# Weight conversion and attention in the first token group of a three-stage kernel: a piece converted within one pair of blocks

## The chip, the cores and the metric

The kernel runs on one core of one Trainium2 chip. The metric is the device time of one execution in microseconds (us), as the median over several runs.

## What is computed

Three stages follow one another; the input is attention's q, k, v (4 batches, 8 heads, 576 rows, head size 64), so 2304 tokens of 512 numbers.

```python
kv = np.einsum('bhsd,bhse->bhde', k, v)
out = np.einsum('bhsd,bhde->bhse', q, kv)
rms = np.sqrt(np.mean(out * out, axis=-1, keepdims=True) + 1e-06)
x = out / rms * g_norm                     # then reshaped to (2304, 512)

h = x @ w_in                               # 512 x 2048
g = h * np.clip(h + 3.0, 0.0, 6.0) / 6.0
x = g @ w_out                              # 2048 x 512

logits = x @ w_gate                        # 8 experts, the largest wins
h = np.maximum(np.einsum('ecd,edf->ecf', disp, w1), 0.0)
y = np.einsum('ecf,efd->ecd', h, w2)       # then weighted by the gate
```

`disp` holds the tokens sorted by expert, 576 places for each. `w_in` and `w_out` come as 64-bit floats, the rest as 32-bit ones.

## The kernel before, in words

**Number format.** A matrix value is split into two 16-bit halves (hi and lo), and a product is three TensorE products (hi·hi, hi·lo, lo·hi). So every weight must first be converted. `w_in` is converted in eight pieces of 256 columns, here called p0 to p7, `w_out` in eight pieces of 256 rows, p8 to p15 (`conv[0]` to `conv[15]` in the code). `f64_piece` (L217) converts one piece in six steps, each a step of a generator: three integer operations on VectorE (DVE; L228, L231, L234) that make a 32-bit float `f` out of the two words of the 64-bit one, then two on ScalarE (ACT; L239 writes the hi half, L241 scales `f` in place), and one on GpSimd (POOL; L243 writes the lo half). After the third step `feed()` issues the next load of a piece on SP's queue (L98). `convert(i, n)` (L621) issues the next n steps of piece i.

**Token groups.** The 2304 tokens go in five groups of 512 (the last has 256). For a group, `mm1` makes 16 blocks h of 128 columns (24 TensorE products of 512 columns for a pair of blocks, L572); `gated` (L575) turns each block into g on three engines: ACT reads the block from PSUM into t (L580), DVE multiplies (L582, g6), ACT writes g's hi half (L584), and POOL its lo half (L585; DVE does it in the later groups). `mm2` (L592) then multiplies g by w_out, 12 products a block and 512 tokens (L600). A pair of blocks f = 2k, 2k+1 of `mm1` needs p(k), one of `mm2` needs p(8+k).

**The first group.** Its code (up to `early.close()`, L698) stands under a manual schedule: each engine executes its instructions in the order in which the code was written. After that only SP's order is manual. In the first group all sixteen pieces are converted, at each even f half of two pieces: DVE's three steps of one piece (`convert(kf + 2, 3)`), and ACT's and POOL's three of the piece whose DVE steps ran a pair earlier (`convert(kf + 1, 3)`), L664 and L665 in the first loop and L685 and L686 in the second. After the first group come the other four groups, which convert nothing of these two matrices, and the experts.

**Attention.** The first 512 rows of batch 0 are done by `first_group` (L322 to L415): TensorE products `o`, ACT's squares, TensorE sums (`ss`), a chain of small DVE operations (L371 to L376), the products `r`, which spread the norms to all rows (L386), and then ACT's `x0T` (L395). `warm` issues products of zeros (L644) for TensorE's clock. All other rows are done by `att_o` (L419) in parts: products `o` (L436), ACT's square (L439), DVE's reduction (L440), DVE's `ms` (L445), ACT's square root (L450), four small DVE operations, DVE's `xs` (L468), ACT's and POOL's `row` (L480, L482), and a transposing DMA on SP (L483). `att_kv` makes the products k·v of a batch in PSUM, `keep_kv` (L306) copies them into the tile `kvbd` on DVE and ACT, `load_kv` and `load_q` issue a batch's loads on SP (L77 to L89).

Of the kernel before, what the change touches and what calls it, by code (L numbers as in the profile page):

```python
# [9 lines left out]
F32 = mybir.dt.float32  # L10
# [6 lines left out]
P = 128  # L17
# [13 lines left out]
def moe_chain(ctx: ExitStack, tc: tile.TileContext, qT, k, v, g_norm, w_in, w_out,  # L31
# [111 lines left out]
    for i in range(P // D):  # L143
        nc.sync.dma_start(gn[i * D : (i + 1) * D, :], g_norm.rearrange("(d o) -> d o", o=1))
    feed(3)
    load_kv(1)


    wg_raw = const.tile([P, NP, E], F32, name="wg_raw")
    nc.sync.dma_start(wg_raw, w_gate.rearrange("(c p) e -> p c e", p=P))  # L150
    bd = const.tile([P, NP, P], F32, name="kvbd")
    nc.gpsimd.memset(bd, 0.0)
    iota = const.tile([P, P], F32, name="iota")
# [12 lines left out]
    for i in range(2):  # L166
# [10 lines left out]
    wg = const.tile([P, NP, 2 * E], F16, name="wg")  # L177
    nc.scalar.activation(wg[:, :, :E], wg_raw, AF.Copy, scale=S_GATE)
    nc.vector.scalar_tensor_tensor(out=wg[:, :, E:], in0=wg_raw, scalar=S_GATE, in1=wg[:, :, :E],
                                   op0=ALU.mult, op1=ALU.subtract)  # L180
    xd = dram.tile([E * CAPP, ROW], F16, name="xd")
# [89 lines left out]
    with ExitStack() as p1:  # L271
# [33 lines left out]

        def keep_kv(ps):  # L306
            nc.vector.tensor_copy(bd[:D, :, :D], ps[:D, :, :D])
            nc.scalar.activation(bd[D:, :, D:], ps[D:, :, D:], AF.Copy)
# [13 lines left out]
        def first_group(w_a, w_b):  # L322
# [23 lines left out]
            for p in range(NP):  # L346
                ps = bank("o")
                nc.tensor.matmul(ps, bd[:, p, :], raws["q", 0, p // 2][:, p % 2, :T], start=True, stop=True)
                sq = sg.tile([P, T], F32, tag="g", name="sq0")
                nc.scalar.activation(sq, ps, AF.Square)  # L350
                banks.append(ps)
                sqs.append(sq)
            for _ in range(3):
                next(w_a)
            ss = bank("ss")
# [7 lines left out]
            nc.scalar.activation(u, ms, AF.Sqrt, bias=eps, scale=1.0 / D)  # L363
            next(w_a)
            next(w_a)
            for p in range(NP):
                oc = sg.tile([P, T], F32, tag="g", name="oc")
                nc.scalar.activation(oc, banks[p], AF.Copy)
                banks[p] = oc
            next(w_a)  # L370
            nc.vector.tensor_scalar(out=ms, in0=ms, scalar1=1.0 / D, scalar2=1.0e-6, op0=ALU.mult, op1=ALU.add)  # L371
# [4 lines left out]
            nc.vector.scalar_tensor_tensor(out=r, in0=q, scalar=-3.0, in1=r, op0=ALU.add, op1=ALU.mult)  # L376
            warm(14)
            warm(16)

# [27 lines left out]
            low(0, x0, nc.vector)  # L407
            low(1, x1, nc.gpsimd)
            x2 = norm(2)
            x3 = norm(3)  # L410
            low(2, x2, nc.vector)
            low(3, x3, nc.gpsimd)
            for _ in range(3):
                next(w_b)
# [4 lines left out]
        def att_o(b, parts, start=0):  # L419

            chunks, s0 = [], start
            while s0 < S:
# [151 lines left out]

        def gated(g, f, ps, eng):  # L575
            n_t = sizes[g]
            sc = S_G / (S_X0 * S_WIN)

            t = sb.tile([P, T], F32, tag="t", name="t")[:, :n_t]
            nc.scalar.activation(t, ps, AF.Relu, bias=b3, scale=sc / (S_X0 * S_WIN))  # L580
            g6 = sb.tile([P, T], F32, tag="g6", name="g6")[:, :n_t]
            nc.vector.scalar_tensor_tensor(out=g6, in0=t, scalar=6.0 * sc, in1=ps, op0=ALU.min, op1=ALU.mult)  # L582
            gt = sg.tile([P, 2, T], F16, tag="g", name="g")
            nc.scalar.activation(gt[:, 0, :n_t], g6, AF.Copy)  # L584
            eng.tensor_tensor(out=gt[:, 1, :n_t], in0=g6, in1=gt[:, 0, :n_t], op=ALU.subtract)  # L585
            gts[g].append(gt)
# [62 lines left out]
        warm(11, wb)  # L649
        keep_kv(att_kv(0, lambda: warm(8, wb)))  # L650
        nc.vector.tensor_scalar(out=gn, in0=gn, scalar1=S_WIN, scalar2=None, op0=ALU.mult)
# [10 lines left out]
        for f in range(NF):  # L662
            kf = f // 2
            if f % 2 == 0:  # L664
                convert(kf + 2, 3)  # L665
                convert(kf + 1, 3)
            if f > 1:
                ps = bank("h")
                mm1_mm(ps, 0, f, range(NP), PAIRS, True, True)
                hs.append(ps)  # L670
            gated(0, f, hs[f], nc.gpsimd)
            if f == 11:
                kv1 = att_kv(1)
            if f > 5 and f % 2 == 1:
                nc.sync.dma_start(*fills.pop(0))
        list(att_o(0, (1,), T))
        load_q(1)
        keep_kv(kv1)
        load_kv(2)
        acc = [bank("x") for _ in range(sizes[0] // P)]  # L680
        att1 = att_o(1, (2, 1, 1, 1))
        for f in range(NF):
            kf = NF // 2 + f // 2
            if f % 2 == 0:
                convert(kf + 2, 3)  # L685
                convert(kf + 1, 3)  # L686
            for j, ps in enumerate(acc):
                mm2(ps, 0, j, range(f, f + 1))
                if f == NF - 1:
                    finish_block(ps, 0, j)  # L690
            if 4 <= f <= 11:
                next(att1)
# [8 lines left out]
        for g in range(1, NG):  # L701
            for f in mm1(g):
# [6 lines left out]
                if f == 10 and g + 1 < B:  # L709
                    keep_kv(att_kv(g + 1))  # L710
                    if g + 2 < B:
# [253 lines left out]
```

## Time and profile before

| what | value |
|---|---|
| median of three runs | 702.54 us (702.40 to 704.43) |
| the profiled execution | 701.1 us |
| its span, first to last instruction | 699.3 us, mean granted TensorE clock 0.987 of full speed |
| TensorE (PE) busy in the span | 656.1 us (94%) |
| DVE, ACT, POOL busy | 340.3, 278.4, 107.3 us |

The first group takes four stretches of the span:

| stretch, us | what runs | PE busy | DVE busy | ACT busy |
|---|---|---|---|---|
| 0 to 31.19 | attention of the first 512 rows | 23.48 | 10.12 | 9.72 |
| 31.19 to 86.39 | `mm1`, with p2 to p9 converted on DVE | 48.72 | 44.54 | 36.92 |
| 86.39 to 146.45 | `mm2`, with p10 to p15 and batch 1's attention | 51.34 | 38.68 | 26.17 |
| 146.45 to 699.30 | groups 1 to 4, experts | 532.55 | 246.97 | 205.59 |

How the rows further down are read. A row of the timeline is: start in us, duration in us, engine, line and operation, tile out<-in with its shape, how many instructions of the kind ran in a row (x), and in brackets how long the engine had been idle and what ended that. PE is TensorE's products, PEld its weight loads, SPq the DMA queue of SP. A row of windows is: start:end, length, then busy us (and instructions) of PE, PEld, DVE, ACT and POOL, the granted clock of TensorE as a share of full speed, DMA's share, GB/s. A row of waits is: who waited, for whom, us in total, how often, the longest.

### The profile page before, as it was taken

What the parts mean: (1) busy time and instruction counts of PE and PEld (TensorE: products, weight loads), DVE (VectorE), ACT (ScalarE), POOL (GpSimd) and SP (SyncE); (2) the same over time, 40 slices, a digit from 0 to 9 for tenths busy, and PEclk for the clock granted to TensorE, in tenths of its full rate; (3) what the DMA queues carried; (4) which work ended last, traced back from release to release, by engine and by line L of the source; (5) the groups of instructions that cost most, each with busy time, mean ns of one, the idle gap of its engine ahead of it and who ended that gap; (6) DMA issues with size and microseconds to landing.
All of it is one profiled execution on the core that took longest, in us unless ns stands there. A gap on an engine that the chain in (4) does not pass through costs nothing. (4 is left out here: it accounts for less than half of the span.)

```text
span 699.3 us, 12621 instructions
## 1 busy us (share of the span) xinstructions
PE 656.1 (94%) x5071; PEld 374.9 (54%) x5071; DVE 340.3 (49%) x786; ACT 278.4 (40%) x433; POOL 107.3 (15%) x112
## 2 busy tenths in 40 slices
PE   7788969899899999999999999988998999999986
PEld 3333525444454445544444448556775766776754
DVE  1687785736582164732553029552134661166262
ACT  2457753535441154410443018431144561166171
POOL 1256652400010110001100011010011010110101
PEclk9989989999999999999999999999999999999998
DMA  9997879470628543362100115509839997089750
GB/s 308 355 265 214 252 247 317 124 202 15 181 62 194 173 131 130 113 143 46 47 16 1 31 45 162 150 24 147 214 71 287 296 211 194 32 196 255 241 109 23
DMA packets 125221, 108.78 MB, mean 156 GB/s; under 512 B 83943, under 2 KB 88551, under 8 KB 125152
## 3 DMA queue, kind: packets, MB, share of 16 engines
q1 hardware_dynamic: 122096, 98.42, 53.5%
q0 software_dynamic: 3056, 9.41, 3.7%
q8 instruction: 47, 0.77, 0.5%
q14 instruction: 22, 0.18, 0.1%
HBM read 64.55 MB, written 25.23 MB: 128 GB/s over the span
## 5 line engine op out<-in xcount | busy, mean ns | idle before, releaser
L572 PE MATMUL h<-x0T,w 128*128 128x512 f16 (+1 forms) x960 | 195.7, 362 | 9.8 <-POOL w L243 5.8
L600 PE MATMUL x<-w,g 128*128 128x512 f16 x864 | 194.1, 383 | 8.7 <-POOL w L243 6.4
L572 PEld LDWEIGHTS <-w 128*128 128x128 f16 x960 | 92.3, 98 | 102.9 <-issue 9.0
L600 PEld LDWEIGHTS <-g 128*128 128x128 f16 x864 | 83.9, 99 | 109.2 <-issue 15.0
L861 PE MATMUL h<-xe,w 128*128 128x128 f16 (+1 forms) x1920 | 107.2, 218 | 8.6 <-PEq L899 3.1
L876 PE MATMUL y<-w,ht 128*128 128x512 f16 (+1 forms) x504 | 112.3, 379 | 1.6 <-DVE ht L785 1.6
L861 PEld LDWEIGHTS <-w 128*128 128x128 f16 x1920 | 104.9, 99 | 15.2 <-issue 9.8
L876 PEld LDWEIGHTS <-ht 128*128 128x128 f16 (+1 forms) x504 | 48.9, 99 | 55.7 <-issue 1.7
L582 DVE SCALAR_TENSOR_TENSOR g<-t,h 128x512 f32<-128x512 f32 (+1 forms) x80 | 50.2, 632 | 40.4 <-ACT t L580 40.4
L866 DVE SCALAR_TENSOR_TENSOR ht<-h,ht 128x512 f16<-128x512 f32 (+1 forms) x40 | 26.5, 663 | 86.7 <-ACT ht L865 86.7
L580 ACT ACTIVATE t<-h,b 128x512 f32<-128x512 f32 (+1 forms) x80 | 51.2, 640 | 36.7 <-PE h L572 36.5
L584 ACT ACTIVATE g<-g 128x512 f16<-128x512 f32 (+1 forms) x80 | 46.2, 585 | 45.7 <-DVE g L582 45.4
L553 POOL DMA_INDIRECT xd<-row,sl x18 | 19.4, 1076 | 280.8 <-DVE sl L551 163.5
L259 DVE SCALAR_TENSOR_TENSOR w<-raw_kv,w 128x1024 f16<-128x1024 f32 x33 | 40.2, 1223 | 32.1 <-ACT w L256 31.5
L585 DVE TENSOR_TENSOR g<-g,g 128x512 f16<-128x512 f32 (+1 forms) x64 | 39.4, 623 | 27.0 <-ACT g L584 26.9
L887 POOL DMA_INDIRECT out<-ysb,ti x21 | 21.2, 1008 | 202.6 <-ACT ysb L886 85.8
L607 DVE SCALAR_TENSOR_TENSOR row<-x,row 128x512 f16<-128x512 f32 x18 | 12.3, 690 | 74.2 <-ACT row L606 74.2
L865 ACT ACTIVATE ht<-h 128x512 f16<-128x512 f32 (+1 forms) x40 | 23.0, 576 | 58.5 <-PE h L861 51.2
L886 ACT ACTIVATE ysb<-y,meta 128x512 f32<-128x512 f32 (+1 forms) x21 | 14.4, 687 | 75.8 <-PE y L876 55.7
L606 ACT ACTIVATE row<-x 128x512 f16<-128x512 f32 x18 | 10.7, 596 | 75.0 <-issue 37.4
L243 POOL TENSOR_TENSOR w<-f,w 128x1024 f16<-128x1024 f32 x16 | 34.1, 2132 | 39.1 <-ACT f L241 39.1
L256 ACT ACTIVATE w<-raw_kv 128x1024 f16<-128x1024 f32 x33 | 34.4, 1048 | 0.9 <-ACTq L899 0.8
(121 smaller groups left out, 462.4 us busy)
## 6 DMA issues: line engine op xcount, KB each, us to landing
raw_kv<-in_w SPq DMA_DIRECT2D x33, 512.0 KB, 7.1
xd<-zero SPq DMA_DIRECT2D x20, 514.0 KB, 8.7
raw_w<-in_w SPq DMA_DIRECT2D x19, 512.0 KB, 6.8
raw_w<-in_w_in SPq DMA_DIRECT2D x8, 1024.0 KB, 9.6
raw_w<-in_w_out SPq DMA_DIRECT2D x8, 1024.0 KB, 9.2
raw_q<-in_w SPq DMA_DIRECT2D x12, 512.0 KB, 6.4
raw_q<-in_qT SPq DMA_DIRECT2D x8, 576.0 KB, 5.3
out<-zero SPq DMA_DIRECT2D x6, 768.0 KB, 5.6
```

The costliest lines, as they stand in the source:

```text
L243: nc.gpsimd.tensor_tensor(out=d[:, 1], in0=f32, in1=d[:, 0], op=ALU.subtract)
L256: nc.scalar.activation(d[:, :, 0, :], r, AF.Copy, scale=scale)
L259: nc.vector.scalar_tensor_tensor(out=d[:, :, 1, :], in0=r, scalar=scale, in1=d[:, :, 0, :], op0=ALU.mult, op1=ALU.subtract)
L572: nc.tensor.matmul(ps, w[:, a, c * 256 + o : c * 256 + o + P], x0T[g][:, b * NP + c, :n_t], start=start and n == 0, stop=stop and n == len ...
L580: nc.scalar.activation(t, ps, AF.Relu, bias=b3, scale=sc / (S_X0 * S_WIN))
L582: nc.vector.scalar_tensor_tensor(out=g6, in0=t, scalar=6.0 * sc, in1=ps, op0=ALU.min, op1=ALU.mult)
L584: nc.scalar.activation(gt[:, 0, :n_t], g6, AF.Copy)
L585: eng.tensor_tensor(out=gt[:, 1, :n_t], in0=g6, in1=gt[:, 0, :n_t], op=ALU.subtract)
L600: nc.tensor.matmul(ps, gts[g][f][:, a, j * P : (j + 1) * P], w[:, b, o : o + DM], start=(f == 0 and i == 0), stop=(f == NF - 1 and i == le ...
L861: nc.tensor.matmul(ps[:, f, :ns], w[c // 2][:, c % 2, a, f * P : (f + 1) * P], xe[:, b * NP + c, :ns], start=(n == 0), stop=(n == 3 * NP - 1))
L866: nc.vector.scalar_tensor_tensor(out=ht[:, 1, :, :ns], in0=ps[:, :, :ns], scalar=0.0, in1=ht[:, 0, :, :ns], op0=ALU.max, op1=ALU.subtract)
L876: nc.tensor.matmul(ps[:ns], hts[q][:, a, f, :ns], w[f // 2][:, f % 2, b, :], start=(n == 0), stop=(n == 3 * NFE - 1))
```

## The change

1. The load of the gate's weights (`wg_raw`) is issued on SP before the first three loads of `w_in`; its conversion (one small ACT and one small DVE instruction) moves from the start of the program to block f = 4 of the first `mm1` loop.
2. There are two tiles `kvbd`, one for even and one for odd batches. So `keep_kv` of batch 1 and the load of batch 2's k and v are issued at f = 11 of that loop, not after it.
3. In `first_group` the six steps of p0 and p1 are issued at other places: two DVE steps of p0 before the chain of norms and the third after it, ACT's first step behind that, the other two between the norms and after them; all six steps of p1 at the end (three before). 18 products of zeros stand ahead of `r` in place of 30.
4. At an even f both loops now issue all six steps of one piece: in the first loop DVE's three first, and ACT's two and POOL's one inside `gated`, behind ACT's t of that block; in the second loop all six in a row.
5. Batch 0's last 64 rows (`att_o(0, (1,), T)`) and the load of batch 1's q move from between the loops to behind block f = 0 of the second one.

```diff
+    wg_raw = const.tile([P, NP, E], F32, name="wg_raw")
+    nc.sync.dma_start(wg_raw, w_gate.rearrange("(c p) e -> p c e", p=P))
     feed(3)
     load_kv(1)
-    wg_raw = const.tile([P, NP, E], F32, name="wg_raw")
-    nc.sync.dma_start(wg_raw, w_gate.rearrange("(c p) e -> p c e", p=P))
-    bd = const.tile([P, NP, P], F32, name="kvbd")
-    nc.gpsimd.memset(bd, 0.0)
+    kvbd = []
+    for i in range(2):
+        t = const.tile([P, NP, P], F32, name=f"kvbd{i}")
+        nc.gpsimd.memset(t, 0.0)
+        kvbd.append(t)
...
-    nc.scalar.activation(wg[:, :, :E], wg_raw, AF.Copy, scale=S_GATE)
-    nc.vector.scalar_tensor_tensor(out=wg[:, :, E:], in0=wg_raw, scalar=S_GATE, in1=wg[:, :, :E],
-                                   op0=ALU.mult, op1=ALU.subtract)
...
-            for _ in range(3):
-                next(w_a)
+            next(w_a)
+            next(w_a)
...
             nc.scalar.activation(u, ms, AF.Sqrt, bias=eps, scale=1.0 / D)
-            next(w_a)
-            next(w_a)
...
-            next(w_a)
...
             nc.vector.scalar_tensor_tensor(out=r, in0=q, scalar=-3.0, in1=r, op0=ALU.add, op1=ALU.mult)
-            warm(14)
-            warm(16)
+            next(w_a)
+            next(w_a)
+            warm(18)
...
             low(1, x1, nc.gpsimd)
+            next(w_a)
             x2 = norm(2)
...
             low(3, x3, nc.gpsimd)
-            for _ in range(3):
+            next(w_a)
+            for _ in range(6):
                 next(w_b)
...
-        def gated(g, f, ps, eng):
+        def gated(g, f, ps, eng, between=None):
...
             nc.scalar.activation(t, ps, AF.Relu, bias=b3, scale=sc / (S_X0 * S_WIN))
+            if between:
+                between()
...
             if f % 2 == 0:
                 convert(kf + 2, 3)
-                convert(kf + 1, 3)
...
-            gated(0, f, hs[f], nc.gpsimd)
+            gated(0, f, hs[f], nc.gpsimd, lambda: f % 2 or convert(kf + 2, 3))
+            if f == 4:
+                nc.scalar.activation(wg[:, :, :E], wg_raw, AF.Copy, scale=S_GATE)
+                nc.vector.scalar_tensor_tensor(out=wg[:, :, E:], in0=wg_raw, scalar=S_GATE, in1=wg[:, :, :E],
+                                               op0=ALU.mult, op1=ALU.subtract)
             if f == 11:
-                kv1 = att_kv(1)
+                keep_kv(1, att_kv(1))
+                load_kv(2)
...
-        list(att_o(0, (1,), T))
-        load_q(1)
-        keep_kv(kv1)
-        load_kv(2)
...
             if f % 2 == 0:
-                convert(kf + 2, 3)
-                convert(kf + 1, 3)
+                convert(kf + 2, 6)
...
+            if f == 0:
+                list(att_o(0, (1,), T))
+                load_q(1)
```

The order in which the engines' instructions stand shows two places. Each row is a line of the code, the operation, and its tile out<-in; the number behind a tile's name tells one buffer's use from the next.

ACT in the first loop, blocks f = 6 and 7, before (`w_155` is p4; `f_518` is the float of p5, which DVE makes during this pair):

```order
L239 ACTIVATE w_155<-f_468,gn_84 128x1024
L241 ACTIVATE f_468<-f_468,gn_84 128x1024
L580 ACTIVATE t_540<-h_527,b3_127 128x512
L584 ACTIVATE g_544<-g6_542 128x512
L580 ACTIVATE t_560<-h_547,b3_127 128x512
L584 ACTIVATE g_564<-g6_562 128x512
L239 ACTIVATE w_156<-f_518,gn_84 128x1024
```

and with the change (`w_156` is p5, and `f_510` its float, made by DVE during this same pair; line numbers are shifted by two to four):

```order
L582 ACTIVATE t_529<-h_516,b3_129 128x512
L239 ACTIVATE w_156<-f_510,gn_84 128x1024
L241 ACTIVATE f_510<-f_510,gn_84 128x1024
L588 ACTIVATE g_536<-g6_534 128x512
L582 ACTIVATE t_552<-h_539,b3_129 128x512
L588 ACTIVATE g_556<-g6_554 128x512
```

ACT's two steps of a piece stood a pair behind DVE's, ahead of both blocks' t; now they stand in DVE's own pair, between the even block's t and everything else of the pair.

DVE over the same pair, with the change; before, the same five kinds stood in the same order:

```order
L228 TENSOR_SCALAR u_509<-raw_w_388 128x1024
L231 SCALAR_TENSOR_TENSOR u_509<-raw_w_388,u_509 128x1024
L234 SCALAR_TENSOR_TENSOR f_510<-raw_w_388,u_509 128x1024
L586 SCALAR_TENSOR_TENSOR g6_534<-t_529,h_516 128x512
L586 SCALAR_TENSOR_TENSOR g6_554<-t_552,h_539 128x512
L228 TENSOR_SCALAR u_560<-raw_w_412 128x1024
```

DVE's own order has not moved; what has is that the odd block's t, which its second g6 reads, now stands on ACT behind the L239 and L241 of the piece that DVE has just finished.

ACT in the second loop, around one part of batch 1's attention, before (`w_163` is p12; DVE has made p13's float `f_1001` just ahead of this part's reduction):

```order
L480 ACTIVATE row0_995<-xs_993 128x512
L239 ACTIVATE w_163<-f_929 128x1024
L241 ACTIVATE f_929<-f_929 128x1024
L439 ACTIVATE sq_1025<-o_1020 128x512
L450 ACTIVATE u_1043<-ms_1040 128x8
```

and with the change (`w_164` is p13):

```order
L482 ACTIVATE row0_987<-xs_985 128x512
L239 ACTIVATE w_164<-f_993 128x1024
L241 ACTIVATE f_993<-f_993 128x1024
L441 ACTIVATE sq_1017<-o_1012 128x512
L452 ACTIVATE u_1035<-ms_1032 128x8
```

Here too the two ACT steps read the float of this pair's piece and not of the last one's, ahead of the part's square and square root.

## Rows read from the trace of the kernel before

**Rows 1.** Windows: the rest of the span after the first group.

```profile
146.45:699.30 552.85, 532.55 (x4390) 316.73 (x4388) 246.97 (x657) 205.59 (x332) 42.55 (x54) 1.00 0.50 128
```

**Rows 2.** Waits of PE, 0 to 200 us.

```profile
PE x L600 <- POOL w L243: 6.4, 5, 3.0
```

**Rows 3.** Timeline of the start, all engines.

```profile
20.89 0.42 DVE L371 TENSOR_SCALAR ss<-ss 128x256 f32<-128x256 f32 x1
...
23.93 0.42 DVE L376 SCALAR_TENSOR_TENSOR rms<-ss,rms 128x256 f32<-128x256 f32 x1
...
30.39 0.23 ACT L178 ACTIVATE wg<-wg_raw 128x32 f16<-128x32 f32 x1 [5.11 <-DMA wg_raw<-in_w_gate]
...
31.19 0.38 PE L572 MATMUL h<-x0T,w 128*128 128x512 f16 x1 [3.35 <-ACT x0T L395]
...
40.39 1.22 DVE L234 SCALAR_TENSOR_TENSOR f<-raw_w,u 128x1024 int32<-128x1024 int32 x1
```

**Rows 4.** Windows on either side of the gate weights' landing.

```profile
22.00:26.00 4.00, 3.88 (x19) 1.62 (x19) 2.25 (x4) 3.25 (x6) 2.13 (x1) 1.00 1.05 386
26.00:30.00 4.00, 1.84 (x16) 1.40 (x17) 0.76 (x2) 0.00 (x0) 0.00 (x0) 1.00 1.09 258
```

**Rows 5.** Timeline of one pair of blocks, first matrix.

```profile
57.47 1.13 ACT L239 ACTIVATE w<-f,gn 128x1024 f16<-128x1024 f32 x1
...
58.70 1.15 ACT L241 ACTIVATE f<-f,gn 128x1024 f32<-128x1024 f32 x1
...
61.25 0.63 ACT L584 ACTIVATE g<-g 128x512 f16<-128x512 f32 x1 [0.82 <-DVE g L582]
...
61.78 0.67 ACT L580 ACTIVATE t<-h,b 128x512 f32<-128x512 f32 x1
...
62.55 0.69 DVE L582 SCALAR_TENSOR_TENSOR g<-t,h 128x512 f32<-128x512 f32 x1 [1.34 <-ACT t L580]
...
63.16 1.22 DVE L228 TENSOR_SCALAR u<-raw_w 128x1024 int32<-128x1024 int32 x1
...
65.69 1.23 DVE L234 SCALAR_TENSOR_TENSOR f<-raw_w,u 128x1024 int32<-128x1024 int32 x1
```

**Rows 6.** Timeline: third steps of pieces p9, p10 and p13 on DVE.

```profile
85.24 1.23 DVE L234 SCALAR_TENSOR_TENSOR f<-raw_w,u 128x1024 int32<-128x1024 int32 x1
...
95.81 1.22 DVE L234 SCALAR_TENSOR_TENSOR f<-raw_w,u 128x1024 int32<-128x1024 int32 x1
...
117.56 1.22 DVE L234 SCALAR_TENSOR_TENSOR f<-raw_w,u 128x1024 int32<-128x1024 int32 x1
```

**Rows 7.** Timeline: attention in the second matrix's stage.

```profile
92.36 0.68 DVE L468 TENSOR_TENSOR xs<-o,r 64x512 f32<-64x512 f32 x1
...
96.39 1.02 SPq L89 DMA_DIRECT2D raw_q<-in_qT  x2
...
108.99 1.95 PE L436 MATMUL o<-kvbd,raw_q 128*128 128x128 f32 x16
...
112.32 0.17 DVE L445 TENSOR_SCALAR ms<-msq 128x16 f32<-128x16 f32 x1
...
117.94 2.13 POOL L243 TENSOR_TENSOR w<-f,w 128x1024 f16<-128x1024 f32 x1 [0.46 <-ACT f L241]
...
119.41 0.69 DVE L445 TENSOR_SCALAR ms<-msq 128x8 f32<-128x8 f32 x1
...
121.92 1.22 DVE L228 TENSOR_SCALAR u<-raw_w 128x1024 int32<-128x1024 int32 x1
```

**Rows 8.** DMA issues, 96.95 to 97.45 us.

```profile
raw_q<-in_qT SPq DMA_DIRECT2D x1, 576.0 KB, 5.0
```

**Rows 9.** Timeline of PE alone: the runs after two waits.

```profile
42.44 12.24 PE L572 MATMUL h<-x0T,w 128*128 128x512 f16 x48 [2.78 <-POOL w L243]
...
141.49 5.12 PE L600 MATMUL x<-w,g 128*128 128x512 f16 x23 [1.27 <-POOL w L243]
```

**Rows 10.** Window inside PE's run after the longest wait of rows 9.

```profile
43.00:44.00 1.00, 1.00 (x4) 0.30 (x2) 0.52 (x1) 0.44 (x1) 1.00 (x1) 0.50 1.03 399
```

More of the change, by code (lines that the diff above doesn't have):

```diff
@@ L304, in att_kv, with keep_kv @@
             return ps
-        def keep_kv(ps):
+        def keep_kv(b, ps):
+            bd = kvbd[b % 2]
             nc.vector.tensor_copy(bd[:D, :, :D], ps[:D, :, :D])
@@ L347, in first_group @@
                 ps = bank("o")
-                nc.tensor.matmul(ps, bd[:, p, :], raws["q", 0, p // 2][:, p % 2, :T], start=True, stop=True)
+                nc.tensor.matmul(ps, kvbd[0][:, p, :], raws["q", 0, p // 2][:, p % 2, :T], start=True, stop=True)
                 sq = sg.tile([P, T], F32, tag="g", name="sq0")
@@ L419, in att_o @@
         def att_o(b, parts, start=0):
+            bd = kvbd[b % 2]
             chunks, s0 = [], start
@@ L649, in moe_chain @@
         warm(11, wb)
-        keep_kv(att_kv(0, lambda: warm(8, wb)))
+        keep_kv(0, att_kv(0, lambda: warm(8, wb)))
         nc.vector.tensor_scalar(out=gn, in0=gn, scalar1=S_WIN, scalar2=None, op0=ALU.mult)
@@ L709, in moe_chain @@
                 if f == 10 and g + 1 < B:
-                    keep_kv(att_kv(g + 1))
+                    keep_kv(g + 1, att_kv(g + 1))
                     if g + 2 < B:
```

## The prediction, made before the change was run

> **What bounds the kernel now.** I read the stage table first. Behind the first group TensorE is busy 532.55 of 552.85 us [rows 1], so what the first group loses or gains reaches the end of the span nearly whole, and no later slack takes it up. The change touches the first group alone. There TensorE is not the bound: it waits for the lo halves of converted pieces, 6.4 us in five waits in the second loop [rows 2] and up to 2.78 us at once in the first [rows 9]. So I read the chain that makes the pieces, in order of time, from the timeline. What counts in the end is when the last piece, p15, is ready: the last 23 products start on it at 141.49 [rows 9].
>
> All times below are of the one profiled execution (701.1 us, 1.4 us or 0.2% under the median).
>
> **The start (items 1 and 3).** TensorE begins `mm1` at 31.19, when ACT has made `x0T`; ACT had stood 5.11 us behind the gate weights' load, whose conversion is ahead of it in ACT's order [rows 3]. That goes. What is late next is the norms with p0's steps among them. In DVE's order two steps of p0 precede the chain of norms, which takes 3.46 us (20.89 to 24.35) [rows 3]. It could start 1.2 us earlier, for the third step is no longer ahead of it, but the gate weights' load now goes ahead of `w_in`'s. Its cost to them has no row of its own. Below it is nothing (the queue has room); above, windows with and without its small packets moved 258 and 386 GB/s over 4 us [rows 4], so at most a third of 4 us, 1.3 us. I take 1.3, because the queue is full at this time, and keep 0 for the range. Then the norms are made at 24.5, DVE's third step of p0 ends at 25.7, ACT's L239 on it 1.15 later at 26.9, and `x0T` some 0.6 behind, as now behind the gate's (30.62 to 31.19): `mm1` begins at 27.5, 3.7 us sooner. The twelve products of zeros less end before the norms do and cost nothing in themselves. The second memset of a `kvbd` is on POOL, which is idle there: nothing. p2's third step, whose place behind `x0T` is unchanged, ends at 38.0 and not at 41.61.
>
> **The first loop (item 4).** Here I expect the loss. Now DVE's third steps of p2 and p9 start 44.85 us apart [rows 3, 6], seven pairs of 6.41. A pair is no chain: ACT's part belongs to a piece finished a pair before, so it can run beside DVE. With the change ACT's L239 must wait for the float that DVE makes in this pair, and everything else of the pair stands behind it on ACT, the odd block's t too, which DVE's second g6 needs; and behind that g6 stands DVE's next piece. That closes a loop through both engines. From the durations of one pair [rows 5]: L239 to L241 1.23; L241 1.15, less the 0.10 by which ACT's next begins before an end, 1.05; the even block's g to the odd block's t 0.53; t to g6 0.77; g6 to the next piece's first step 0.61; the three steps 3.76 (63.16 to 66.92). Sum 7.95, so 1.54 more for each of seven pairs, 10.8. Add about 0.35 for `keep_kv`, now in this loop (it left the second, where it is paid now), and 0.25 for the gate's conversion (its two instructions take 0.42; some lies beside DVE; 0 to 0.42). p9's third step ends at 38.0 + 55.65 + 0.6 = 94.25; now it ends at 86.47 [rows 6]: 7.8 later. TensorE itself needs 5.34 for a pair's 24 products at 0.223 each [rows 9] and waits for the blocks to be taken up, so it isn't the bound. Bounds of the period: 6.41, if ACT's part found room beside the rest, and 8.6, if one more of the two t (0.67) came into the loop. I take the sum, for each of its links is fixed by the written order.
>
> **The second loop (items 4 and 5).** The last 64 rows of batch 0 stand between p9 and p10 now, and between p10 and p11 with the change. So p10's third step ends one period of 7.95 behind p9's, at 102.2 (now 97.03 [rows 6]), 5.2 later, and those rows are still to come. A part of attention with a piece ahead of it becomes a longer chain too: ACT's square stands behind L239 and L241 of the piece that DVE has just made, and DVE's `ms` behind the square. Worked out: L239 1.23, L241 1.15, 0.08 to POOL's start, POOL's L243 2.13 (DVE's `ms` comes out only with POOL's end, see below), 1.82 from there to the next piece's first step (120.10 to 121.92), 3.76 for it [rows 5, 7]: 10.2. Now it is 6.9 from p13's third step to p14's (117.56 to 121.92 + 2.53 [rows 5 to 7]), since ACT's and POOL's steps there are of an older piece and are done sooner. Bounds: 6.9 and 10.2; what the order makes each engine wait for is plain, so I take the upper.
> So p11's float is made at 112.4 and p12's at 116.2. Batch 1's q is loaded behind the transposes of these 64 rows: `xs` at about 108.0, just ahead of p11's first step (112.4 - 3.76 = 108.6), 4.03 later the load is issued (92.36 to 96.39) at 112.0 and 112.5, 5.0 later it has landed, at 117.5 [rows 7, 8]. So the first products `o` of batch 1 end at 119.0 instead of 110.94, 8.1 later [rows 7]. p13's third step follows as now 7.84 behind (110.94 to 118.78 [rows 6, 7]) at 126.8; p14's and p15's each 10.2 later, 137.0 and 147.2. ACT and POOL finish p15 4.6 us later, at 151.8; here the change wins something, since p15's second half needn't wait for the next pair. The last 23 products start at 151.8 instead of 141.49: 10.3 later. While TensorE waits, it now does eleven of `mm1`'s products for the next group, instead of one: 10 x 0.223 = 2.2 us done already.
>
> **The sum.** 10.3 - 2.2 = 8.1, taken as 8.0 us slower: 709.1 on the profiled execution's scale, 710.5 on the median's. The path is: -3.7 at the start, +7.8 at p9, +8.1 at batch 1's first products, +10.3 at p15, -2.2.
>
> **POOL and DVE together.** DVE's `ms` on 16 numbers a row took 0.17 us with POOL idle, and 0.69 on 8 numbers with POOL's L243 beside it, and it ended at 120.10, with POOL's end at 120.07 [rows 7]. I take it that it always waits for POOL's end.
> The Trainium skill, "SBUF — State Buffer", section on SBUF's two separate sides, says why it would: the two engines share a pair of ports, and one that holds it shuts the other out for its whole instruction. The row agrees. By that rule the part costs 10.2; with DVE's step running beside POOL's it would cost about 9.4, with the sum at 5.5 (first rival).
>
> **The rivals.**
> *No wait for POOL in the new order.* The small DVE operations may land ahead of POOL's start or pass it. Then each of three parts (p11, p14, p15) is 0.8 shorter: 2.5 us, 708. For it: the 0.17 row; against: the 0.69 row, with ACT's square ahead of both. 0.15.
> *The granted clock.* After 2.78 us without work TensorE's granted clock was 0.50 of full speed, the 1.2 GHz level, and 48 products took 12.24 us, where 48 x 0.223 are 10.7 [rows 9, 10]: 1.5 lost. In the new order it waits longer for batch 1's q (the sixteen products of 1.95 would take twice that) and before the last 23 products (again about 1.7): 3.6 on top, 714. For it: that row; against: 23 products behind 1.27 us of idle ran at full rate. 0.23.
> *Faster.* The pair holds: if L239 and L241 fit into the time in which ACT now waits, and the period stays 6.41, then each loop is as now, p15 is ready in its own pair, and the start's 3.7 stays: 698.8. What decides is the period of L234, below 6.9 for faster. Against it is that all links of the loop are of engines that run in written order. 0.07.
> *No difference.* The loss of both loops and the gains at both ends cancel, or waits in the next group take it up: 702.5. Against it: 532.55 of 552.85. 0.05.
>
> **The numbers.** My forecast has 0.50: 710.5, of its own between 708.5 and 712.5. The range: down to 705.0, for the case without POOL's wait (708), with a load that costs the start nothing (1.3) and a period short of the sum by 0.25 in seven pairs (1.75); up to 715.0, for the clock. Outside it stay the faster and the unchanged case, 0.12. A difference under 0.3%, 2.1 us, can't be told from none. Slower by more: 0.50 + 0.15 + 0.23 = 0.88; faster 0.07; same 0.05.
>
> **What would show it.** The first `mm1` product at 27.5. In the first loop starts of L234 about 7.95 us apart, ACT's L241 directly behind L239 with the even block's g behind it, and idle times of TensorE of about 2.6 us in a pair. Products `o` of batch 1 waiting for the DMA of q until about 117.5. In the second loop, pieces about 10 us apart where a part of attention lies between, and `ms` ending with L243. The last 23 products at about 152. I am wrong if L234 starts are under 7 us apart; if TensorE's first-group end is later by under 2 us though the chain is as I say, the credit for `mm1`'s products was too small or the wait elsewhere.

## The result and the profile after

The changed kernel is slower: 711.58 us (median of 20 runs) against 702.44 us for the kernel before (20 runs); the ratio is 1.012, with a 95% interval from 1.0096 to 1.0144, so 8.4 us on 702.44 (6.7 to 10.1). The ratio and its interval leave out the two slowest runs of the changed kernel, over 1.5% above its fastest, so the ratio isn't quite the quotient of the two medians. The profiled execution took 709.66 us, with a span of 707.9 against 699.3.

| place | before | forecast | after |
|---|---|---|---|
| first product of the first loop starts | 31.19 | 27.5 | 25.61 |
| p2's third step ends | 41.61 | 38.0 | 35.88 |
| p9's third step ends | 86.47 | 94.25 | 92.64 |
| p10's third step ends | 97.03 | 102.2 | 100.42 |
| first products `o` of batch 1 end | 110.94 | 119.0 | 119.69 |
| p13's third step ends | 118.78 | 126.8 | 127.49 |
| p15's third step ends | 133.44 | 147.2 | 147.42 |
| last 23 products of the second loop start | 141.49 | 151.8 | 151.85 |

The waits of TensorE from 0 to 200 us (who waited, for whom: us in total, times, longest). One row from before, for the first loop:

```profile
PE h L572 <- POOL w L243: 5.8, 4, 2.8
```

In the changed kernel:

```profile
PE h L574 <- POOL w L243: 11.6, 6, 2.8
PE o L438 <- DMA raw_q<-in_qT: 8.1, 2, 7.3
PE x L604 <- POOL w L243: 6.2, 4, 3.0
```

Before, the wait for POOL's L243 came to 6.4 us in the second loop [rows 2]; it is 6.2 now, and the same wait in the first loop, 5.8 us before, is now the largest one with 11.6. The wait for q's load is new. Since TensorE can only wait where something is late, this view tells where to look and not which of them is the cause: the experiments show that of the 8.1 us for q only a small part counts.

The start of the changed kernel, from its timeline (start, duration, engine, line, tile, [idle before and what ended it]):

```profile
16.86 1.24 DVE L228 TENSOR_SCALAR u<-raw_w 128x1024 int32<-128x1024 int32 x1 [2.14 <-DMA raw_w<-in_w_in]
...
22.30 0.42 DVE L374 SCALAR_TENSOR_TENSOR rms<-ss,rms 128x256 f32<-128x256 f32 x1
22.64 1.21 DVE L234 SCALAR_TENSOR_TENSOR f<-raw_w,u 128x1024 int32<-128x1024 int32 x1
...
22.87 2.00 PE L385 MATMUL r<-rms,back 64*128 64x256 f32 x16 [0.51 <-DVE rms L374]
...
25.61 0.38 PE L574 MATMUL h<-x0T,w 128*128 128x512 f16 x1 [0.74 <-ACT x0T L394]
```

The norms are ready at 22.72 (before 24.35, [rows 3]); DVE's third step of p0 runs behind them, beside the products `r`, and the first product starts at 25.61 with nothing of the gate's weights ahead of it.

One pair of blocks of the first loop after the change, from the end of p5's float to that of p6's; the same kinds of rows stood in [rows 5]:

```profile
59.43 1.22 DVE L234 SCALAR_TENSOR_TENSOR f<-raw_w,u 128x1024 int32<-128x1024 int32 x1
60.57 0.68 DVE L586 SCALAR_TENSOR_TENSOR g<-t,h 128x512 f32<-128x512 f32 x1
...
60.69 1.15 ACT L239 ACTIVATE w<-f,gn 128x1024 f16<-128x1024 f32 x1 [2.45 <-DVE f L234]
...
61.93 1.15 ACT L241 ACTIVATE f<-f,gn 128x1024 f32<-128x1024 f32 x1
62.98 0.61 ACT L588 ACTIVATE g<-g 128x512 f16<-128x512 f32 x1
...
63.50 0.67 ACT L582 ACTIVATE t<-h,b 128x512 f32<-128x512 f32 x1
64.27 0.69 DVE L586 SCALAR_TENSOR_TENSOR g<-t,h 128x512 f32<-128x512 f32 x1 [3.02 <-ACT t L582]
64.88 1.22 DVE L228 TENSOR_SCALAR u<-raw_w 128x1024 int32<-128x1024 int32 x1
...
67.40 1.22 DVE L234 SCALAR_TENSOR_TENSOR f<-raw_w,u 128x1024 int32<-128x1024 int32 x1
```

This is the loop of the prediction, link by link. DVE's float ends at 60.65; ACT's L239 stands at it (idle 2.45 before, ended by DVE); L241 at 61.93; the even block's g at 62.98; the odd block's t at 63.50; DVE's g6, which had waited 3.02 us for that t, at 64.27; and DVE's next piece at 64.88. From L234 to L234 it is 7.97 us.

Batch 1's first products, and then one part of attention between p14 and p15:

```profile
110.12 1.03 SPq L89 DMA_DIRECT2D raw_q<-in_qT  x2
...
114.72 1.19 PE L438 MATMUL o<-kvbd,raw_q 128*128 128x128 f32 x4 [7.28 <-DMA raw_q<-in_qT]
...
116.76 2.93 PE L438 MATMUL o<-kvbd,raw_q 128*128 128x128 f32 x12 [0.85 <-DMA raw_q<-in_qT]
...
136.24 1.22 DVE L234 SCALAR_TENSOR_TENSOR f<-raw_w,u 128x1024 int32<-128x1024 int32 x1
...
137.49 1.06 ACT L239 ACTIVATE w<-f 128x1024 f16<-128x1024 f32 x1 [3.02 <-DVE f L234]
...
139.72 2.13 POOL L243 TENSOR_TENSOR w<-f,w 128x1024 f16<-128x1024 f32 x1 [4.01 <-ACT f L241]
...
140.86 1.01 DVE L447 TENSOR_SCALAR ms<-msq 128x8 f32<-128x8 f32 x1
...
146.20 1.22 DVE L234 SCALAR_TENSOR_TENSOR f<-raw_w,u 128x1024 int32<-128x1024 int32 x1
```

A row of windows beside the products on q's second half, with the granted clock third from its end:

```profile
116.00:118.00 2.00, 1.24 (x6) 1.24 (x7) 0.00 (x0) 0.44 (x1) 1.48 (x1) 0.50 1.09 390
```

From p14's third step to p15's are 9.96 us, with DVE's `ms` on 8 numbers taking 1.01 us beside L243 and ending with it (141.87 and 141.85). The end of the first group on TensorE:

```profile
151.85 5.12 PE L604 MATMUL x<-w,g 128*128 128x512 f16 x23 [0.56 <-POOL w L243]
156.81 8.36 PE L574 MATMUL h<-x0T,w 128*128 128x512 f16 x38
```

### The profile page after: what moved, and what is told of

It is laid out like the page before. It is cut to its first block, busy times and chain, and to the rows that moved or that the text cites. A ratio compares the mean times of both kernels' runs of the same rounds, so it can differ in the third digit from the quotient of the medians.

```text
span 707.9 us, 12602 instructions
## 1 busy us (share of the span) xinstructions
PE 654.8 (92%) x5059; PEld 375.1 (53%) x5059; DVE 342.9 (48%) x786; ACT 277.8 (39%) x433; POOL 106.4 (15%) x113
## 5 line engine op out<-in xcount | busy, mean ns | idle before, releaser
L574 PE MATMUL h<-x0T,w 128*128 128x512 f16 (+1 forms) x960 | 196.5, 362 | 15.0 <-POOL w L243 11.6
L243 POOL TENSOR_TENSOR w<-f,w 128x1024 f16<-128x1024 f32 x16 | 34.0, 2126 | 51.1 <-ACT f L241 51.1
```

The source lines that it names most:

```text
L243: nc.gpsimd.tensor_tensor(out=d[:, 1], in0=f32, in1=d[:, 0], op=ALU.subtract)
L574: nc.tensor.matmul(ps, w[:, a, c * 256 + o : c * 256 + o + P], x0T[g][:, b * NP + c, :n_t], start=start and n == 0, stop=stop and n == len ...
```

## Experiments

**One loop at a time, then both.** x1 puts the first loop's pieces back over two pairs (ACT's two steps and POOL's one stand behind the odd block's g), x2 the second loop's, x3 does both; all else stays as changed.

```diff
x1:
-            gated(0, f, hs[f], nc.gpsimd, lambda: f % 2 or convert(kf + 2, 3))
+            gated(0, f, hs[f], nc.gpsimd)
...
+            if f % 2:
+                convert(kf + 2, 3)
x2:
-                convert(kf + 2, 6)
+                convert(kf + 2, 3)
...
             if f % 2 == 1:
+                convert(kf + 2, 3)
                 nc.sync.dma_start(*fills.pop(0))
```

x1, expected: 

> The changed kernel with the first loop's pieces split over two pairs again (ACT's and POOL's steps behind the odd block's g), all else as changed. Closed-loop theory (ACT's L239 and L241 in front of the odd block's t make a loop with DVE): L234 starts 6.35 us apart again instead of 7.95; p9's third step ends at about 81.4 instead of 92.64; the parts of the second loop stay 10 us apart; the last 23 products start at about 138 instead of 151.85, span about 694. Rival 'the late load of q is the loss': q's load still stands behind the 64 rows, TensorE still waits some 8 us for it, the time stays within 2 us of 708. Rival 'POOL and DVE share a port and that stretches the pair': the period stays above 7.5, since POOL's work is the same.

x1 measured 698.76 us, ratio 0.9944 (0.9924 to 0.9963): faster than the kernel before. p9's third step ended at 81.22 and the last 23 products started at 138.94; the span was 693.7. TensorE still waited 6.1 us for q. Two third steps of x1 on DVE with the gate's conversion between them:

```profile
47.18 1.22 DVE L234 SCALAR_TENSOR_TENSOR f<-raw_w,u 128x1024 int32<-128x1024 int32 x1
...
49.87 1.19 DVE L677 SCALAR_TENSOR_TENSOR wg<-wg_raw,wg 128x32 f16<-128x32 f32 x1 [0.81 <-ACT wg L676]
...
54.09 1.22 DVE L234 SCALAR_TENSOR_TENSOR f<-raw_w,u 128x1024 int32<-128x1024 int32 x1
```

The pairs around this one are 6.34 us long (40.84 to 47.18); this one is 6.91 long, since the gate's DVE step takes 1.19 here. The long period of the changed kernel thus comes from where ACT's two steps (and POOL's one behind them) stand: the same instructions give 6.34. The rival with q falls, since TensorE still waits 6.1 us for it and the time is gone; so does the one with the port alone, since POOL's work is the same and the period is not.

x2, expected: 

> The changed kernel with the second loop's pieces split over two pairs again, the first loop as changed. Closed-loop theory: p9 ends at 92.6 as in the changed kernel, pieces with a part of attention between are 6.9 to 7.8 us apart instead of 10.0; the last 23 products start at about 146 instead of 151.85, span 702 to 705. Rival 'the late load of q is the loss': the load is issued a few us earlier only, TensorE still waits for it 5 us or more and the span is above 706.

x2 measured 706.34 us, ratio 1.0064 (1.0035 to 1.0092), span 703.4. Its third steps of p13, p14 and p15:

```profile
120.84 1.22 DVE L234 SCALAR_TENSOR_TENSOR f<-raw_w,u 128x1024 int32<-128x1024 int32 x1
...
127.60 1.22 DVE L234 SCALAR_TENSOR_TENSOR f<-raw_w,u 128x1024 int32<-128x1024 int32 x1
...
134.50 1.22 DVE L234 SCALAR_TENSOR_TENSOR f<-raw_w,u 128x1024 int32<-128x1024 int32 x1
```

They are 6.8 and 6.9 us apart, not 10.0; the span lies in the 702 to 705 forecast. The last 23 products started at 143.79, 2 us sooner than I had said, since the products of batch 1 did not wait for q at all: they ended at 114.2, for TensorE got there late by itself.

x3, expected: 

> Both loops split again; what is left of the change is the start, the two kvbd tiles, the gate's conversion in the loop and the 64 rows with q's load inside the second loop. Closed-loop theory: p9 ends at about 81.4, parts 6.9 to 7.8 apart, the last 23 products start at about 133, before TensorE's own work would reach it (about 127 to 131); span about 691, faster than the kernel before by 8 us (1.2%). Rival 'q's load' : span above 700, since the 64 rows and the load behind them still come late in the second loop.

x3 measured 693.73 us, ratio 0.9872 (0.9831 to 0.9912), span 691.2. TensorE's timeline:

```profile
100.97 1.60 PE L438 MATMUL o<-kvbd,raw_q 128*128 128x128 f32 x12 [1.27 <-DMA raw_q<-in_qT]
...
132.16 5.12 PE L604 MATMUL x<-w,g 128*128 128x512 f16 x23 [1.49 <-POOL w L243]
```

So what is left of the change without the two new orders makes the kernel 9 us faster, and the two orders cost more than that: by the ratios 17.4 us together, 12.4 for the first loop alone and 3.9 for the second alone; by the spans of the profiled executions 16.7, 14.2 and 4.5. The first loop has the larger part either way. Whether the two costs overlap can't be told: by the ratios the parts add up to a little less than the whole, by the spans to a little more. q still ends last ahead of p13: TensorE waits for it 1.8 us in two waits, of which the row shows the second.

**The late load of q.** x4 is the changed kernel with one more move:

```diff
-                list(att_o(0, (1,), T))
+                a0 = att_o(0, (1,), T)
+                next(a0)
                 load_q(1)
+                list(a0)
```

Expected: 

> The changed kernel with batch 1's q loaded right behind the products of the 64 rows and ahead of their transposes on SP; nothing else moved. Closed-loop theory: TensorE's wait for q (8.1 us in two waits) goes, the first products of batch 1 end at about 109.4 instead of 119.69, but p13 then waits for its own chain: its third step ends at about 125.0 instead of 127.49, p14 and p15 follow 10 us apart, the last 23 products start at about 149.4, span about 705.4, 2.5 less. Rival 'the late load of q is the loss': the 8.1 us of waiting come back, span about 700.

x4 measured 706.73 us, ratio 1.0061 (1.0041 to 1.0081). TensorE in x4:

```profile
108.33 1.60 PE L438 MATMUL o<-kvbd,raw_q 128*128 128x128 f32 x12 [0.60 <-DMA raw_q<-in_qT]
...
120.71 1.77 PE L438 MATMUL o<-kvbd,raw_q 128*128 128x128 f32 x8 [3.37 <-DVE xs L470]
...
149.17 5.12 PE L604 MATMUL x<-w,g 128*128 128x512 f16 x23 [0.34 <-POOL w L243]
```

The first products of batch 1 ended at 109.93, 9.8 us sooner than in the changed kernel, and p13's third step at 124.81, 2.7 sooner; the last 23 products started 2.7 sooner. TensorE now waited for DVE instead, 3.37 us. This is a wait off the chain in its largest part: of 8.1 us that TensorE waited for q, some 2.7 were worth something at the end of the first group. By the ratios the gain is 4.1 us (1.0061 against 1.012; their intervals leave 1.1 to 7.2). The profiled execution, the longest of the five runs of x4, had a span of 709.2 even so, because behind the first group it took 555.1 us against 551.1; of that, 0.9 is the wait for the transposes of the gate's rows and 0.9 that for the experts' first load, the rest I could not assign. The code behind the first group is the same in all these kernels, and still this stretch took 551.4 us in x5 and 555.5 in x9 (both below), which both enter it with none of the next group's products done. So two spans that differ by a few us say little about the first group; the times within it, and the ratios, say more.

The same move on x3 is x5.

Expected: 

> Both loops split again and batch 1's q loaded ahead of the transposes of the 64 rows. In the kernel with both loops split the products of batch 1 waited 1.8 us for q and the last 23 products started at 132.16. Theory (with the loops open, q's load is the link that ends last ahead of p13): p13's third step ends 3 to 4 us earlier (about 107 instead of 110.42), and with it p14, p15 and the last 23 products (about 128.5); span about 687.5 instead of 691.2. Rival (p13 then waits for p12 on ACT and POOL): less than 1.5 us.

x5 measured 690.04 us, ratio 0.9866 (0.9824 to 0.9908), span 686.2. TensorE in x5:

```profile
36.87 12.21 PE L574 MATMUL h<-x0T,w 128*128 128x512 f16 x48 [2.74 <-POOL w L243]
...
98.35 1.95 PE L438 MATMUL o<-kvbd,raw_q 128*128 128x128 f32 x16
...
129.86 5.12 PE L604 MATMUL x<-w,g 128*128 128x512 f16 x23 [1.49 <-POOL w L243]
```

The first products of batch 1 no longer wait. The last 23 products start 2.3 us sooner than in x3, short of the forecast 3 to 4 and above the rival's 1.5. By the ratios x5 and x3 cannot be told apart.

**Small steps of DVE beside POOL.** x6 moves the gate's load back behind batch 1's k and v, and its conversion ahead of block 4's t:

```diff
     feed(3)
     load_kv(1)
+    wg_raw = const.tile([P, NP, E], F32, name="wg_raw")
+    nc.sync.dma_start(wg_raw, w_gate.rearrange("(c p) e -> p c e", p=P))
...
+            if f == 4:
+                nc.scalar.activation(wg[:, :, :E], wg_raw, AF.Copy, scale=S_GATE)
+                nc.vector.scalar_tensor_tensor(out=wg[:, :, E:], in0=wg_raw, scalar=S_GATE, in1=wg[:, :, :E],
+                                               op0=ALU.mult, op1=ALU.subtract)
             gated(0, f, hs[f], nc.gpsimd, lambda: f % 2 or convert(kf + 2, 3))
```

Expected: 

> The changed kernel with two moves: the gate weights' load back behind batch 1's k and v on SP, and their conversion ahead of block 4's t instead of behind its g. (1) Start: if the load ahead of w_in's costs w_in something, p0's first step, at 16.86 in the changed kernel, starts up to 1.3 us earlier; if not, within 0.3 us of it. (2) The pair of blocks 4 and 5, 8.92 us long in the changed kernel against 7.95 of its neighbours: the conversion's DVE step took 1.57 us beside POOL's L243 and ended with it. Theory (a small DVE step waits for POOL's end): in its new place POOL has nothing to do, the step takes 0.2, the pair 7.95 us, all that follows is 1.0 earlier, the last 23 products start at about 150.9. Rival (the two instructions themselves are the cost): the pair stays at 8.3 or more.

In the changed kernel the conversion stood here:

```profile
54.23 2.12 POOL L243 TENSOR_TENSOR w<-f,w 128x1024 f16<-128x1024 f32 x1 [3.60 <-ACT f L241]
...
54.83 1.57 DVE L677 SCALAR_TENSOR_TENSOR wg<-wg_raw,wg 128x32 f16<-128x32 f32 x1 [2.50 <-ACT wg L676]
```

and in x6, on DVE:

```profile
16.78 1.25 DVE L228 TENSOR_SCALAR u<-raw_w 128x1024 int32<-128x1024 int32 x1 [2.17 <-DMA raw_w<-in_w_in]
...
50.47 1.22 DVE L234 SCALAR_TENSOR_TENSOR f<-raw_w,u 128x1024 int32<-128x1024 int32 x1
51.60 0.18 DVE L676 SCALAR_TENSOR_TENSOR wg<-wg_raw,wg 128x32 f16<-128x32 f32 x1
...
58.43 1.22 DVE L234 SCALAR_TENSOR_TENSOR f<-raw_w,u 128x1024 int32<-128x1024 int32 x1
```

The same DVE instruction takes 1.57 us beside L243, with both ending at 56.35 to 56.40, and 0.18 where POOL has nothing to do. The pair is 7.96 long instead of 8.92, and p9's third step ends 1.0 sooner (91.64). The last 23 products start at 151.04, 0.8 sooner. p0's first step starts at 16.78, against 16.86 in the changed kernel. One pair of starts is not much, but in the ten profiled executions that have the gate's load ahead of those of `w_in` this step starts between 16.28 and 17.48, and in the two that have it behind (before and x6) at 17.19 and 16.78: a cost of 1.3 us isn't there, one of a few tenths could not be seen. The time of x6, 707.71 us in its one run, lies among those of the changed kernel (704.79 to 717.45).

x7 takes L243 of p10 to p15 out of the way of `ms`:

```diff
-                convert(kf + 2, 6)
+                convert(kf + 2, 5)
...
             if f % 2 == 1:
+                convert(kf + 2, 1)
                 nc.sync.dma_start(*fills.pop(0))
```

Expected: 

> The changed kernel with POOL's L243 of p10 to p15 issued behind the part of attention that follows it, not ahead of it. Theory (DVE's ms waits for the end of POOL's L243): ms takes 0.17 us instead of 1.00, third steps with a part between (p10 to p11, p13 to p14, p14 to p15) come 9.1 us apart instead of 10.0, while the pieces themselves become ready some 5 us later behind their third step. Rival (ms takes 1 us for another reason, such as its semaphore): still 10.0 apart.

DVE in x7, p13's and p14's third steps and the `ms` between them:

```profile
124.22 1.22 DVE L234 SCALAR_TENSOR_TENSOR f<-raw_w,u 128x1024 int32<-128x1024 int32 x1
...
128.92 0.17 DVE L447 TENSOR_SCALAR ms<-msq 128x8 f32<-128x8 f32 x1
...
133.43 1.22 DVE L234 SCALAR_TENSOR_TENSOR f<-raw_w,u 128x1024 int32<-128x1024 int32 x1
```

`ms` takes 0.17 us, and the third steps are 9.21 us apart (9.19 from p14 to p15), where they were 9.97 and 9.96. So `ms` does wait for POOL's end and this is worth 0.8 us a part. The kernel as a whole isn't faster for it (712.92 us in its one run), since the pieces become ready later behind their third steps: TensorE waits 15.6 us for L243 in the second loop instead of 6.2, and the last 23 products start at 154.07.

**The products of zeros.** x10 has `warm(30)` in place of `warm(18)`.

Expected: 

> The changed kernel with 30 products of zeros ahead of r, as before, in place of 18. The prediction put the twelve less at nothing. In the changed kernel the 18 end at 22.36 and the norms at 22.72, so by the same rate (0.226 each) 30 would end at 25.1: r would start at 25.1 instead of 22.87 and the first product of the first loop 2.2 us later, near 27.8, with p2's third step behind it. Rival (the start is bound by p0's steps on ACT and DVE): r is later, but the first product stays within 0.7 us of 25.61.

TensorE in x10:

```profile
15.67 1.95 PE L359 MATMUL ss<-sq,hsum 128*64 128x256 f32 x16
17.55 6.65 PE L648 MATMUL warm<-zero,ones 128*128 128x512 f16 x30
24.13 2.00 PE L385 MATMUL r<-rms,back 64*128 64x256 f32 x16
26.83 0.38 PE L574 MATMUL h<-x0T,w 128*128 128x512 f16 x1 [0.70 <-ACT x0T L394]
```

The 30 end at 24.20 and `r` starts at 24.13, straight behind them. In this run everything up to the sums had come 0.75 sooner than in the changed kernel (15.67 against 16.42), so counted from there the first product is 11.16 us away instead of 9.19: 2.0 later. Of the 5.6 us that the changed kernel wins at the start, these twelve products are 2.0; they were no cover that could be had for nothing. The rival, a first product within 0.7 us of 25.61, falls. (The time, 713.90 us in one run, lies within those of the changed kernel.)

**A version that beats both.** x8 joins x5 and x6's place for the conversion, with p15 alone converted whole in its pair; x9 is the same with the conversion behind the last piece (and no longer at block 4).

```diff
x9, on top of x5:
-                convert(kf + 2, 3)
+                convert(kf + 2, 6 if f == 10 else 3)
...
+            if f == 13:
+                nc.scalar.activation(wg[:, :, :E], wg_raw, AF.Copy, scale=S_GATE)
+                nc.vector.scalar_tensor_tensor(out=wg[:, :, E:], in0=wg_raw, scalar=S_GATE, in1=wg[:, :, :E],
+                                               op0=ALU.mult, op1=ALU.subtract)
             if f % 2 == 1:
-                convert(kf + 2, 3)
+                if f < 11:
+                    convert(kf + 2, 3)
```

x8, expected: 

> Both loops split, q early, the gate's conversion ahead of block 4's t, and p15 alone converted whole within its pair (nothing stands behind it). Theory: 0.6 to 1.0 us from the gate's place, and p15 ready about 4.5 us behind its third step instead of 8, so that the last 23 products start when TensorE gets to them, at 125 to 127.5; span about 686, 13 us (1.9%) less than before. Rival (ACT's steps of p15 hold back the last part of attention and with it the next group's first blocks): no better than with q early alone.

x8 measured 692.29 us, ratio 0.9871 (0.9839 to 0.9903), span 692.0 where 686 was forecast: no better than x5. In the split order POOL's L243 (51.00 to 53.13) is at work where the conversion now stands, so its DVE step took 1.62 us, to 53.18, and the pair 7.81. And in the profiled execution the start was late:

```profile
13.38 6.63 PE L349 MATMUL o<-raw_q,kvbd 128*128 128x512 f32 x8 [0.98 <-ACT kvbd L309]
```

The eight products `o` took 6.63 us, where the changed kernel's and x5's took 3.70, and all that follows came 3 us later. Counted from the first product, TensorE reached the end of the first group in 108.3 us against 109.1 in x5.

x9, expected: 

> Both loops split, q early, p15 alone converted whole in its pair, and the gate's conversion put behind the last piece (block 13 of the second loop), where no chain runs through DVE. Theory: the first loop's pair of blocks 4 and 5 comes down from 6.93 to 6.35, p9's third step and all behind it 0.6 earlier; p15 no longer waits for the last part of attention; the last 23 products start at about 128.3 (129.86 with q early alone), span about 685, 14 us (2%) under the kernel before. Rival (TensorE's own work is the bound by then): no more than 0.6.

x9 measured 690.44 us, ratio 0.9835 (0.9802 to 0.9868), span 688.6 where 685 was forecast. TensorE at the end of the first group:

```profile
122.91 10.30 PE L604 MATMUL x<-w,g 128*128 128x512 f16 x47 [0.61 <-POOL w L243]
133.06 20.88 PE L574 MATMUL h<-x0T,w 128*128 128x512 f16 x96
```

p13's third step ended only 0.1 us sooner than in x5: the pair of blocks 4 and 5 came down to 6.35, but the next one was 6.76 long, for which the trace names no cause. The last two blocks of products no longer wait for p15: 47 products run in one go, and the first group ends on TensorE at 133.06, 1.8 us sooner than in x5 and 13.4 sooner than before. Its ratio is the lowest of all kernels run, but the interval overlaps those of x3 and x5, so which of the three is best is not settled; all three are faster than the kernel before by over 0.8%.

## Why the prediction was right, point by point

The median came out 1.1 us above the forecast of 710.5, and the path that the prediction named is the one in the trace. That the number is so close is in part luck: the chain was 1.6 us ahead of the forecast at p9 and 1.9 at the `xs` of batch 0's last rows, and q then came late and was worked through slowly by 2.6, so that p15 is only 0.2 off.

- **The start, -3.7 forecast, -5.6 measured.** The term that was mis-sized is the gate weights' load: I took 1.3 us of delay for `w_in`, the upper bound; x6 shows nothing like it, and the lower bound was nearer the truth. Another 0.3 is that `w_in` landed sooner in this profiled execution than in that of the kernel before (16.86 and 17.19), within what it varies by. The twelve products of zeros less were worth 2.0 (x10). The forecast counted on them, as it let `r` start with the norms, but put them at nothing, and that was wrong: 30 would have ended behind the norms. POOL was not idle for the second memset of a `kvbd` either: what follows on POOL starts 0.46 later (`iota` at 1.85 instead of 1.39), which reached no step of the chain.
- **The first loop, 7.95 a pair forecast.** Measured are 7.89, 7.96, 7.97, 7.96 and 7.77 in pairs with nothing else in them, 8.29 with `keep_kv` (0.33; I had 0.35), and 8.92 with the gate's conversion. For that one I had taken 0.25 and 0 to 0.42 as bounds; it was 0.97, outside them, because its DVE step falls beside POOL's L243. I had the row that says so (`ms` [rows 7]) and used it for `ms` alone. x1 shows the mechanism: with ACT's steps behind the pair the period is 6.34. DVE's wait for the odd block's t is 1.34 before [rows 5] and 3.02 now, 1.7 more, which is the added period to within 0.1.
- **The second loop.** p10 came 7.78 behind p9, p11 10.0 behind p10. `xs` to q's load was 4.03 as forecast (106.09 to 110.12). The second half of q landed at 116.76, some 6 us behind its issue, where I had 5.0, and the twelve products on it took 2.93 us, where at the full rate they would have taken about 1.5 (1.95 for sixteen). So the 1.9 us by which the chain was ahead of the forecast were lost again, and `o` ended 0.7 later than said: a near hit out of two misses. From there p13 followed at 7.8, p14 and p15 at 9.97 and 9.96 (forecast 10.2; its two ACT steps are shorter in this loop, 1.06 and not 1.15).
- **POOL and DVE.** That DVE's `ms` waits for POOL's end is shown by x7. The rival without that wait (708) falls.
- **The clock.** The rival came half true. TensorE had nothing to do for 7.28 us ahead of q, and the products behind that ran at a granted clock of 0.50, the 1.2 GHz level (the row of windows in the section on the result); the last 23 ran at 1.00 (5.12 us for 23). What it cost was about the 1.5 us of those twelve products.
- **The end.** The last 23 products start 10.36 us later; eleven products of the next group are done by then instead of one (3 and 8 of them between 148.5 and 151.3), 2.2 us. That makes 8.1; the span grew by 8.6. In the rest the wait for the transposes of the gate's rows is 0.7 longer (2.0 against 1.3), but 0.5 is less than this stretch varies by between executions (x4), so what made it stays open.
- **Faster** failed where it was said to: the first loop's period was above 7.7 throughout. **No difference** failed as well: the ratio's whole interval lies above 1, and the stretch behind the first group was only 1.8 us shorter.

## What to carry to other kernels

Where engines run in written order, count the loop through all of them, not each engine's work: a step that a second engine takes in the same round, ahead of something that the first engine's next round needs, joins the loop with its whole length, though neither engine is near full (from p2 to p9 DVE was busy 63% of the time and ACT 58%). The period grows by that length less what the first engine can do beside it: here the two steps take 2.3 us (60.69 to 62.98), DVE's even g6 of 0.68 runs beside them, and the period grew by 1.6. Let the second engine take the piece of the round before. Converting only the last piece in one round, behind which nothing stands, ended the first group 1.8 us sooner in x9 than in x5; whether the whole kernel gains by it is not shown. And read a wait at its end: TensorE's wait of 8.1 us for q was worth about 2.7, while ACT's steps in the first loop, for which TensorE hardly waited by name, were worth 12 or more.

## What the runs showed of the hardware that I had not expected

A small VectorE operation on two operands (32 numbers a row) is held by a GpSimd operation as `ms` is: 1.57 us against 0.18. VectorE's large integer steps are not: they took 1.22 us with and without L243 beside them (p2's third step, 34.66 to 35.88, ran wholly beside an L243 of 34.53 to 36.66).
The Trainium skill, "SBUF — State Buffer", section on SBUF's two separate sides, limits the lock to operations of VectorE that have two operands in SBUF or run in a mode that uses both ports, and that fits the two cases: the gate's conversion reads both its operands from SBUF, while the integer steps read or write their intermediate result `u` in PSUM and have one operand in SBUF. `ms` has a single operand, so by that page it would have to run in such a mode; no run here shows in which mode it ran.

TensorE's granted clock after a wait is not told by the length of the wait: after 2.75 us without work 48 products took 10.53 us in the changed kernel, and after 2.74 us they took 12.21 in x5 (above). From 37 to 40 us it was 1.00 in the one and 0.50 in the other, the 2.4 and the 1.2 GHz level. The order of the code doesn't tell either: x2 has the changed kernel's first loop unaltered, waits the same 2.75 us, and had 0.50 from 37 to 40. The changed kernel's row:

```profile
36.72 10.53 PE L574 MATMUL h<-x0T,w 128*128 128x512 f16 x48 [2.75 <-POOL w L243]
```

And it can move a whole start: in x8 `o` took 6.63 us instead of 3.70, at 0.50 from 13 to 17 us where x5 had 1.00, behind a wait for k and v of 1.40 us where x5 had 0.44. What decides between them, these runs don't tell. The Trainium skill, "TensorE: Matmul & The Clock Gate", Part 1, says that the chip looks at TensorE's activity in a rhythm of its own that no kernel starts, so that the same kernel can come out either way; the changed kernel and x2 agree with that and don't prove it.
